# The last stores of a one-core attention and feed-forward kernel, issued in row parts, and its last block copied out by two engines

## The chip, the core and the metric

The kernel runs on one core of a Trainium2 chip. A core has five engines with an instruction queue each: TensorE (PE, matrix products; its weight loads are shown as PEld), VectorE (DVE), ScalarE (ACT), GpSimd (POOL) and SyncE (SP), which computes nothing here and only waits and issues transfers. Sixteen DMA engines move data between the core's buffers and the memory on the chip (DRAM). Engines wait for each other, and for transfers, on semaphores. The metric is the device time of one execution in microseconds (us); lower is better.

## The reference

Two stages follow one another (batch 4, 8 heads, 768 positions, head size 64). First a block-sorted attention, then a feed-forward layer with a squared ReLU over 3072 tokens:

```
P = sort_net, five times normalised by rows and by columns (after exp)
k_sorted, v_sorted = P @ blocks of k, P @ blocks of v
attn_out = softmax(q @ k_sorted.T / 8) @ v_sorted        # within each block of 96
x = attn_out as [3072 tokens, 512]
out = relu(x @ w_in) ** 2 @ w_out                        # w_in [512, 2048], w_out [2048, 512], out [3072, 512] f32
```

## The kernel before, in words

A planner (`Plan`) collects all operations with costs and due times, simulates the engines' queues and emits each engine's instructions in the order that it found. A wait between instructions of two engines is put in by the framework, which follows who reads and writes each buffer. Transfers issued by SP count up on eight semaphores in turn, named DMAHW0 to DMAHW7: the first transfer takes DMAHW0, the ninth takes it again. At the end of the program SP waits for all of them in that order, one or two semaphores to an instruction, and then all engines meet.

The part that matters is the end of the feed-forward layer. The tokens of one batch (768) are two groups of 384. `Group.up` makes the hidden layer of a group, 128 hidden units at a time. The second product (hidden layer times `w_out`) is done for the last batch in three pairs of 128-token blocks. A `Pair` multiplies a 2x2 block matrix by Strassen's scheme in Winograd's form: seven products instead of eight, each of eight matmuls (`product`), numbered by `step(k)` with k = 1, 2, 5, 6, 3, 7, 4, between sums and evictions on DVE and ACT. The first pair of a batch (here P) runs among the `up` steps. The other two, A and B, run last, in this order of steps:

```
steps("1A 2A 1B 2B 5A 6A 5B 6B 3A 7A 3B 7B 4A 4B", A=Pair((g1, 2), (g2, 0)),
      B=Pair((g2, 1), (g2, 2), last=b == B - 1))
```

A name such as 5B below is the product of step 5 of pair B. The sums that a pair needs are in DVE's queue (line 1178), the evictions at lines 1210, 268 and 270.

Each product goes into one of four PSUM banks (bank_71 to bank_74), and a bank is taken again when its eviction is done. A pair fills two output buffers of 128 rows by 512 columns in f32, `o1` for its upper row block and `o2` for its lower one. There are four of them, `ob0` to `ob3` (in the built program ob_166 to ob_169), taken in turn: P has ob_168 and ob_169, A has ob_166 and ob_167, and B has ob_168 and ob_169 again. Before an engine writes into a buffer of the turn before, it waits until the old store from it has landed.

The evictions that the text names: `c11` and `c12` (left and right half of `o1`, after steps 2 and 3), `c22` (right half of `o2`, after step 7) and `c21` (left half of `o2`, after step 4, the last product of a pair). Step 4 adds onto the bank that `c22` has just read, so product 4B waits for `c22` of B; 5B is written into the bank that `c11` of B has emptied. `put` stores a buffer when both halves are there; for the last pair (`last`) the two halves of `o2` are stored apart.

Of the kernel before, what the change touches and what calls it, by code (L numbers as in the profile page):

```python
# [59 lines left out]
X_PE = {1: (0, 1, 2, 3), 2: (0, 1, 2, 3)}  # L60

FIRST_MIX = ("0T 1T 2T 1A 3T 2A 6A 5A 7A 3A 4A", "0T 1T 2T 1A 3T 2A 6A 5A 7A 3A 4A")
PRIO = {"evict": -3, "relu": -2, "square": -1, "sum": 0.5, "T1": 0, "T2": 0.3, "T3": 0.6, "T4": 0.7}


# [129 lines left out]
def kernel(  # L195
# [12 lines left out]
    B, H, S, D = q.shape  # L208
# [8 lines left out]
    d_model = moe_w_in.shape[0]  # L217
# [20 lines left out]
    banks = [psb.tile([128, 512], FP32, name=f"bank{n}") for n in range(4)]  # L238
# [11 lines left out]
    plan = Plan()  # L250
# [15 lines left out]
    def copy(eng, out, in_):  # L266
        if eng == "ACT":
            nc.scalar.copy(out=out, in_=in_)  # L268
        else:
            nc.vector.tensor_copy(out=out, in_=in_)  # L270
# [131 lines left out]
    while w >= 4:  # L402
        dst = {C0: mask, 4: mask_t}.get(w)
        if dst is None:
            dst = const.tile([128, w], BF16, name=f"fold{w}")
# [161 lines left out]
    class Unit:  # L567


        def __init__(self, b, hp, halves):  # L570
            self.b, self.hp, self.halves = b, hp, halves
            self.turned = []
            self.tiled = in_tiles(b, 1, HP * (hp // 2))
            self.n, self.old = rks.take()
            if self.tiled:
                self.ksT = kvT_r[self.n][:, 0, :]
                self.i0, self.ni, self.full = 0, NB, True
                return
            self.kvT = kvT_r[self.n]
            self.ksT, self.vsT = self.kvT[:, 0, :], self.kvT[:, 1, :]  # L580
            self.i0, self.ni = NQ * halves[0], NQ * len(halves)
            self.full = len(halves) == 2
# [455 lines left out]
    ob_r = [const.tile([128, d_model], FP32, name=f"ob{n}") for n in range(4)]  # L1038

    def store(so, dst, src, deps, parts=(slice(0, 128),)):  # L1040
        for p in parts:
            sp = plan.add("SP", 0.55, lambda e, p=p: nc.sync.dma_start(out=dst[p, :], in_=src[p, :]),
                          deps)
        rob.use(so, plan.add("WAY", 1.5, lambda e: None, [sp], tail=0.6))
# [8 lines left out]
    NH2, DH = NT // 2, d_model // 2  # L1053
# [15 lines left out]
    def make_t():  # L1069
# [7 lines left out]
        for h in range(2):  # L1077
            done = []
            for name, dst, x, y in (("T1", T1, B12, B11), ("T2", T2, B22, T1),
# [6 lines left out]
                    readers[0] + lands + dep))  # L1086
                done[-1].prio = PRIO[name]
                tsum.setdefault(name, []).append(done[-1])
# [20 lines left out]
    class Group:  # L1109
# [9 lines left out]
        def up(self, nt):  # L1119
# [6 lines left out]
            def mm(e):  # L1126
# [9 lines left out]
                out=h1_r[:, s1, :], in_=banks[n][:, 0:HS], func=AF.Relu), [pe] + old1)  # L1136
            r.prio = PRIO["relu"]
            fb.use(n, pe, r)
# [20 lines left out]

    class Pair:  # L1160

        def __init__(self, top, low, last=False):
            (g1, m1), (g2, m2) = top, low
            x1, x2 = slice(128 * m1, 128 * (m1 + 1)), slice(128 * m2, 128 * (m2 + 1))
            self.gs, self.last = (g1, g2), last
            self.row1, self.row2 = g1.t0 + x1.start, g2.t0 + x2.start
            A11, A12 = g1.h2[:, 0:NH2, x1], g1.h2[:, NH2:, x1]
            A21, A22 = g2.h2[:, 0:NH2, x2], g2.h2[:, NH2:, x2]
            self.ns, olds = rs3.take()
            S3 = s3_r[self.ns]  # L1170
            self.S = (A11, A12, A21, A22, S3)
            nk, oldk = rkeep.take()
            self.nk = nk
            (self.P1s, d1), (self.U2s, d2), (self.P5s, d5) = keep_r[3 * nk:3 * nk + 3]
            self.oldk = oldk + d1 + d2 + d5

            def add(dst, x, y, op, deps):
                o = plan.add("DVE", 0.68, lambda e: nc.vector.tensor_tensor(  # L1178
                    out=dst, in0=x, in1=y, op=op), deps)
                o.prio = PRIO["sum"]  # L1180
                return o

            self.s3 = add(S3, A11, A21, ALU.subtract, g1.sq[0:NH2] + g2.sq[0:NH2] + olds + readers[0]
                          + [units[1, hp].k_op for hp in range(2) if self.ns == 1])
            self.s1 = add(A21, A21, A22, ALU.add, [self.s3] + g2.sq)
            self.add = add
            self.ops = {}
            self.o1, old1 = rob.take()
            self.o2, old2 = rob.take()
            self.oldo = {1: old1, 2: old2}  # L1190
# [14 lines left out]
        def evict(self, n, dst, deps, other=None):  # L1205
# [7 lines left out]
            fb.use(n, op)  # L1213
            return op

        def step(self, k):
            A11, A12, A21, A22, S3 = self.S
            top, low = (slice(0, DH), slice(DH, d_model))
            o = self.ops
            if k == 1:  # L1220
                self.a, old = fb.take()
                o[1] = self.product(A11, B11, self.a, self.gs[0].sq[0:NH2] + old, True)
                self.p1 = self.evict(self.a, self.P1s, [o[1]] + self.oldk)
                self.s2 = self.add(A11, A21, A11, ALU.subtract, [self.s1, self.s3, o[1]])
            elif k == 2:
                self.b, old = fb.take()
                o[2] = self.product(A12, B21, self.b, self.gs[0].sq + old, True)
                self.c11 = self.evict(self.b, ob_r[self.o1][:, top], [o[2], self.p1] + self.oldo[1],
                                      self.P1s)
                fb.release(self.b)  # L1230
                self.s4 = self.add(A12, A12, A11, ALU.subtract, [self.s2, o[2]])
            elif k == 5:
                self.b, old = fb.take()
                o[5] = self.product(A21, T1, self.b, [self.s1] + tsum["T1"] + old, True)
                self.p5 = self.evict(self.b, self.P5s, [o[5]] + self.oldk)
            elif k == 6:
                o[6] = self.product(A11, T2, self.a, [self.s2, self.p1] + tsum["T2"], False)
                self.u2 = self.evict(self.a, self.U2s, [o[6]] + self.oldk)
            elif k == 3:
                o[3] = self.product(A12, B22, self.b, [self.s4, self.p5], False)  # L1240
                self.c12 = self.evict(self.b, ob_r[self.o1][:, low], [o[3], self.u2], self.U2s)
                fb.release(self.b)
                rkeep.use(self.nk, self.c12)
                self.put(self.o1, self.row1, [self.c11, self.c12], ())
            elif k == 7:
                o[7] = self.product(S3, T3, self.a, [self.s3, self.u2] + tsum["T3"], False)
                rs3.use(self.ns, o[7])
                self.c22 = self.evict(self.a, ob_r[self.o2][:, low], [o[7], self.p5] + self.oldo[2],
                                      self.P5s)
                rkeep.use(self.nk, self.c22)  # L1250
            else:
                o[4] = self.product(A22, T4, self.a, [self.c22] + tsum["T4"], False)
                self.c21 = self.evict(self.a, ob_r[self.o2][:, top], [o[4]])
                fb.release(self.a)
                self.put(self.o2, self.row2, [self.c22, self.c21], (low, top))

        def put(self, so, row, ops, halves):
            dst = out[row:row + 128, :]
            if self.last and halves:
                for x, op in zip(halves, ops):  # L1260
                    store(so, dst[:, x], ob_r[so][:, x], [op])
            else:
                store(so, dst, ob_r[so], ops)

    class Tile:

# [25 lines left out]
    def steps(names, **pairs):  # L1292
        for k in names.split():
            pairs[k[1]].step(int(k[0]))

    def ffn_first():

        make_t()
        for half in range(2):
            g = Group(half)  # L1300
            for nt in range(NT):
                g.up(nt)
            steps(FIRST_MIX[half], T=Tile(g, 2 if half == 0 else 0),
                  A=Pair((g, 0), (g, 1)) if half == 0 else Pair((g, 1), (g, 2)))
        fb.release(3)

    def ffn_batch(b):
        g1, g2 = Group(2 * b), Group(2 * b + 1)
        for nt in range(NT):
            g1.up(nt)  # L1310
        nt = 0
        for k in (None, 1, 2, 5, 6, 3, 7, 4, None):
            for _ in range(3 if nt == 0 else 2):
                if nt < NT:
                    g2.up(nt)
                    nt += 1
            if k == 1:
                p = Pair((g1, 0), (g1, 1))
            if k:
                p.step(k)  # L1320
        steps("1A 2A 1B 2B 5A 6A 5B 6B 3A 7A 3B 7B 4A 4B", A=Pair((g1, 2), (g2, 0)),
              B=Pair((g2, 1), (g2, 2), last=b == B - 1))

    qops = {}
# [3 lines left out]
    for k in range(2):  # L1328
        op = plan.add("DVE", 0.42, lambda e, k=k: p_last(e, k), [step])
# [15 lines left out]
    for name in FIRST.split():  # L1345
        stage, n = name[0], int(name[1])
# [82 lines left out]
    fb = Banks((f_slot[0], f_slot[1], 3 - f_slot[0] - f_slot[1]))  # L1429
# [44 lines left out]
```

## Time and profile before

| | us |
|---|---|
| time, median of 3 runs | 212.22 (212.06 to 214.27) |
| time of the profiled execution | 214.04 |
| span of the profiled execution, first to last instruction | 212.3 |
| PE busy in the span | 205.9 (97%) |
| last product on PE, and last copy after it | 206.98 + 1.91, then 208.92 + 0.37 |
| last store issued on SP | 209.32 |

The profile is of one execution, whose own time is 1.74 us more than its span and 1.82 us more than the median of the other runs. Times inside it are us from the start of its span. A row of a timeline gives start, duration, engine, line, operation and what it writes and reads; a number in brackets at its end is the idle time of the engine before it and what ended it. The names of buffers are without their numbers there (ob for ob0 to ob3).

### The profile page before, as it was taken

The numbers are of one execution on the slowest core, as the hardware profiler recorded it, in microseconds if no ns is written. First come the engines' busy times: TensorE is split into PE (matmuls) and PEld (weight loads), VectorE is DVE, ScalarE is ACT, GpSimd is POOL, SyncE is SP. The second block draws the span as 40 slices with busy tenths as digits, with TensorE's granted clock in tenths as the row PEclk, the third lists the DMA queues.
The fourth block names the chain that finished last, engine by engine and source line by source line (L and its number), as shares of the span: only waits on it lengthen the run. The fifth ranks groups of instructions, "written<-read, shape, count | busy, mean of one in ns | idle before, by whom it ended". The sixth has DMA issues, their size and how long they took to land.

```text
span 212.3 us, 5721 instructions
## 1 busy us (share of the span) xinstructions
PE 205.9 (97%) x2337; PEld 143.7 (68%) x2340; DVE 141.2 (67%) x309; ACT 150.4 (71%) x307; POOL 30.8 (15%) x57
## 2 busy tenths in 40 slices
PE   8999999999999999999999999989999999999993
PEld 2467666576566865566779955556789865677882
DVE  5849589974779846867798747677879314633920
ACT  4578799548994549999884089999672189887321
POOL 7957222000019000000720000000000000000000
PEclk9999999999999999999999999999999999999999
DMA  6999999999697994299599768953432420001113
GB/s 142 218 202 208 204 207 211 192 220 280 158 195 134 202 252 85 65 173 185 153 183 229 147 225 113 190 134 96 64 115 40 136 99 0 3 0 49 53 49 148
DMA packets 42266, 30.57 MB, mean 144 GB/s; under 512 B 21696, under 2 KB 37312, under 8 KB 42240
## 3 DMA queue, kind: packets, MB, share of 16 engines
q0 software_dynamic: 12224, 13.24, 37.6%
q1 hardware_dynamic: 30016, 16.97, 33.7%
q8 instruction: 18, 0.29, 0.5%
q14 instruction: 8, 0.07, 0.1%
HBM read 29.70 MB, written 8.72 MB: 181 GB/s over the span
## 4 chain that ended last, share of the span: by engine, by line
PE 89%; ACT 4%; DMA 2%; DVE 2%; issue 1%; ACTq 0%; POOLq 0%
PE bank L1128 36%; PE bank L1195 31%; PE p L945 4%; PE p L718 3%; PE bank L1278 3%; PE p L476 2%; DMA qb<-in_q_dram 2%; ACT h_r L1135 2%; PE p L806 2%; DVE h L1152 1%; PE bank L597 1%; PE bank L998 1%; PE bank L768 1%; PE bank L644 1%; PE p L680 1%
## 5 line engine op out<-in xcount | busy, mean ns | idle before, releaser
L1128 PE MATMUL bank<-xT,w_in_bf 128*128 128x384 bf16 x506 | 90.7, 326 | 0.0
L1128 PEld LDWEIGHTS <-w_in_bf 128*128 128x128 bf16 x506 | 47.1, 98 | 29.1 <-issue 1.4
L1135 ACT ACTIVATE h_r<-bank 128x384 f32<-128x384 f32 x128 | 59.8, 497 | 8.2 <-PE bank L1128 7.1
L1195 PEld LDWEIGHTS <-h 128*128 128x128 bf16 x528 | 50.1, 98 | 9.1 <-issue 1.0
L1152 DVE TENSOR_TENSOR h<-h_r 128x768 bf16<-128x768 f32 x28 | 26.6, 957 | 20.2 <-ACT h_r L1135 20.1
L1195 PE MATMUL bank<-w_out_bf,h 128*128 128x256 bf16 x264 | 33.1, 273 | 0.1
L1150 ACT ACTIVATE h<-h_r 128x768 bf16<-128x768 f32 x36 | 30.6, 851 | 0.9
L749 ACT ACTIVATE et<-p 96x384 bf16<-96x384 f32 x48 | 22.2, 504 | 2.9 <-PE p L718 2.9
L956 DVE TENSOR_TENSOR ao<-p,rec 96x512 bf16<-96x512 f32 x32 | 22.0, 687 | 1.1
L1178 DVE TENSOR_TENSOR h<-h 128x1024 bf16<-128x1024 bf16 x30 | 20.1, 684 | 0.7 <-ACT h L1150 0.5
L1195 PE MATMUL bank<-qb,h 128*128 128x256 bf16 x132 | 17.9, 272 | 0.0
L268 ACT COPY ob<-bank 128x256 f32<-128x256 f32 (+1 forms) x11 | 4.5, 411 | 18.6 <-PE bank L1195 17.4
L268 ACT COPY qT<-bank 128x256 f32<-128x256 f32 (+1 forms) x22 | 8.9, 413 | 10.5 <-PE bank L1195 7.9
L1210 DVE TENSOR_TENSOR ob<-bank,kvT 128x256 f32<-128x256 f32 x18 | 7.6, 424 | 10.5 <-PE bank L1195 9.0
L945 PEld LDWEIGHTS <-et 96*128 96x128 bf16 x256 | 11.1, 97 | 2.8 <-issue 0.7
L268 ACT COPY kvT<-bank 128x256 f32<-128x256 f32 x14 | 5.2, 371 | 10.1 <-PE bank L1195 10.1
L476 PE MATMUL p<-ones 128*128 128x512 bf16 (+1 forms) x28 | 10.2, 524 | 1.1 <-DVE ones L294 1.1
L1195 PE MATMUL bank<-vb,h 128*128 128x256 bf16 x88 | 11.1, 273 | 0.0
L1210 DVE TENSOR_TENSOR ob<-bank,qT 128x256 f32<-128x256 f32 x15 | 6.2, 422 | 7.2 <-PE bank L1195 5.8
L1412 POOL COPY held<-kx 1x1 bf16<-1x1 bf16 x6 | 1.7, 286 | 58.3 <-DMA kx<-kn 58.3
L718 PEld LDWEIGHTS <-kvT 64*128 64x128 bf16 x256 | 6.4, 94 | 5.4 <-issue 4.2
L945 PE MATMUL p<-vblk,et 96*128 96x65 bf16 x192 | 8.9, 193 | 0.0
(109 smaller groups left out, 227.1 us busy)
## 6 DMA issues: line engine op xcount, KB each, us to landing
out_dram<-ob SPq DMA_DIRECT2D x23, 256.0 KB, 2.2
v_way<-vn SPq DMA_DIRECT2D x6, 396.0 KB, 4.9
vblk<-v_way SPq DMA_DIRECT2D x6, 396.0 KB, 4.1
vb<-in_v_dram POOLq DMA_DIRECT2D x6, 384.0 KB, 11.5
kb<-in_k_dram POOLq DMA_DIRECT2D x6, 384.0 KB, 10.3
qb<-in_q_dram POOLq DMA_DIRECT2D x6, 384.0 KB, 12.9
w_in_bf<-in_moe_w_in_dram POOLq DMA_DIRECT2D x4, 512.0 KB, 12.2
w_out_bf<-in_moe_w_out_dram POOLq DMA_DIRECT2D x4, 512.0 KB, 15.7
```

Source lines behind the costliest of these rows:

```text
L268: nc.scalar.copy(out=out, in_=in_)
L476: nc.tensor.matmul(out=p2[slot][:, 0, 0:128 * r].rearrange("p (r x) -> p r x", r=r), lhsT=ones, rhs=ones[:, None, :].to_broadcast([128, r, ...
L749: nc.scalar.activation(out=et[:, h, 0:HS].rearrange("p (n c a) -> p n c a", c=C0, a=NA), in_=st["p"][0:96, h, 0:HS].rearrange("p (n a c) - ...
L945: nc.tensor.matmul(out=oup[:, h, 66 * n:66 * n + D + 1], lhsT=et_r[u.et[hf]][:, h, BLK * n:BLK * n + 128], rhs=(u.vs[:, NQ * hf + n, h, 0: ...
L956: nc.vector.tensor_tensor(out=u.ao[:, n0:n0 + NQ, :, :].rearrange("p n e d -> p e n d"), in0=ov[:, :, :, 0:D], in1=rec[:, :, :, None].to_b ...
L1128: nc.tensor.matmul(out=banks[n][:, 0:HS], lhsT=w_in_bf[:, kc, 128 * nt:128 * (nt + 1)], rhs=xT[:, kc, t0:t0 + HS], start=(kc == 0), stop=( ...
L1135: r = plan.add("ACT", cost_f(HS)[0], lambda e: nc.scalar.activation(out=h1_r[:, s1, :], in_=banks[n][:, 0:HS], func=AF.Relu), [pe] + old1)
L1150: nc.scalar.activation(out=h2, in_=h1, func=AF.Square)
L1152: nc.vector.tensor_tensor(out=h2, in0=h1, in1=h1, op=ALU.mult)
L1178: o = plan.add("DVE", 0.68, lambda e: nc.vector.tensor_tensor(out=dst, in0=x, in1=y, op=op), deps)
L1195: nc.tensor.matmul(out=banks[n][:, 0:DH], lhsT=a[:, j, :], rhs=b[j] if isinstance(b, list) else b[:, j, :],  start=(start and j == 0), sto ...
L1210: op = plan.add("DVE", cost_f(DH)[1], lambda e: nc.vector.tensor_tensor(out=dst, in0=src, in1=other, op=ALU.add), deps)
```

## The change

For the last batch, the stores of P go out in three row parts each (42, 43 and 43 rows), and the store of A's `o1` in two (64 and 64 rows); A's `o2` and B's stores stay as they were. That is five transfers more, so the last store takes DMAHW7 where it took DMAHW2. The last eviction of the kernel (`c21` of B, 128 rows by 256 columns) is written as two copies of 128 columns, one for ACT and one for DVE.

```
+LAST_PARTS = (3, 3), (2, 1)
...
-        def __init__(self, top, low, last=False):
+        def __init__(self, top, low, last=False, parts=(1, 1)):
...
+        def last_evict(self, deps):
+            ops = []
+            for e, x in (("ACT", slice(0, DH // 2)), ("DVE", slice(DH // 2, DH))):
+                ops.append(plan.add(e, 0.28, lambda e, x=x: copy(
+                    e, ob_r[self.o2][:, x], banks[self.a][:, x]), deps))
+                ops[-1].prio = PRIO["evict"]
+            fb.use(self.a, *ops)
+            return ops
...
-                self.c21 = self.evict(self.a, ob_r[self.o2][:, top], [o[4]])
+                if self.last:
+                    c21 = self.last_evict([o[4]])
+                else:
+                    c21 = [self.evict(self.a, ob_r[self.o2][:, top], [o[4]])]
...
+            n = self.parts[so == self.o2]
+            store(so, dst, ob_r[so], ops + more,
+                  [slice(128 * i // n, 128 * (i + 1) // n) for i in range(n)])
...
-                p = Pair((g1, 0), (g1, 1))
+                p = Pair((g1, 0), (g1, 1), parts=LAST_PARTS[0] if b == B - 1 else (1, 1))
...
+              A=Pair((g1, 2), (g2, 0), parts=LAST_PARTS[1] if b == B - 1 else (1, 1)),
```

In SP's queue the stores of the last batch stood as follows, at the end of the program. ob_168 and ob_169 are first those of P, and further down those of B; ob_166 and ob_167 are A's. Of the waits of a row the first is for the semaphore that the transfer itself will count on.

```order
L1042 DMA out_dram<-ob_168 128x512 [waits DMAHW4_49,DVE_49]
L1042 DMA out_dram<-ob_169 128x512 [waits DMAHW5_49,DVE_49]
L1042 DMA out_dram<-ob_166 128x512 [waits DMAHW6_49,DVE_49]
L1042 DMA out_dram<-ob_168 128x512 [waits DMAHW7_49,DVE_49]
L1042 DMA out_dram<-ob_169 128x256 [waits DMAHW0_49,DVE_49]
L1042 DMA out_dram<-ob_167 128x512 [waits DMAHW1_49,Activation_49]
L1042 DMA out_dram<-ob_169 128x256 [waits DMAHW2_49,Activation_49]
```

The same place of SP's queue in the changed kernel:

```order
L1043 DMA out_dram<-ob_168 42x512 [waits DMAHW4_49,DVE_49]
L1043 DMA out_dram<-ob_168 43x512 [waits DMAHW5_49]
L1043 DMA out_dram<-ob_168 43x512 [waits DMAHW6_49]
L1043 DMA out_dram<-ob_169 42x512 [waits DMAHW7_49,DVE_49]
L1043 DMA out_dram<-ob_169 43x512 [waits DMAHW0_49]
L1043 DMA out_dram<-ob_169 43x512 [waits DMAHW1_49]
L1043 DMA out_dram<-ob_166 64x512 [waits DMAHW2_49,DVE_49]
L1043 DMA out_dram<-ob_166 64x512 [waits DMAHW3_49]
L1043 DMA out_dram<-ob_168 128x512 [waits DMAHW4_49,DVE_49]
L1043 DMA out_dram<-ob_169 128x256 [waits DMAHW5_49,DVE_49]
L1043 DMA out_dram<-ob_167 128x512 [waits DMAHW6_49,Activation_49]
L1043 DMA out_dram<-ob_169 128x256 [waits DMAHW7_49,DVE_49]
```

No row is moved; three rows have become eight, and the last row waits for DVE instead of ACT (called Activation in these rows) and counts on DMAHW7.

The end of DVE's queue before: `c11` of B into ob_168, a sum, `c12` of A (into ob_166), `c22` of A (ob_167), `c12` of B and `c22` of B (ob_169).

```order
L1210 TENSOR_TENSOR ob_168<-bank_73,kvT_88 128x256 [waits DMAHW4_49,PE_49,Activation_49]
L1178 TENSOR_TENSOR h_1_165<-h_1_165 128x8x128 [waits DVE_49]
L1210 TENSOR_TENSOR ob_166<-bank_74,qT_84 128x256 [waits PE_49,Activation_49]
L1210 TENSOR_TENSOR ob_167<-bank_71,qT_85 128x256 [waits DMAHW3_49,PE_49]
L1210 TENSOR_TENSOR ob_168<-bank_73,kvT_96 128x256 [waits PE_49,Activation_49]
L1210 TENSOR_TENSOR ob_169<-bank_72,kvT_104 128x256 [waits DMAHW5_49,PE_49]
```

The same place in the changed kernel:

```order
L1211 TENSOR_TENSOR ob_168<-bank_73,kvT_88 128x256 [waits DMAHW5_49,DMAHW4_49,DMAHW6_49,PE_49,Activation_49]
L1179 TENSOR_TENSOR h_1_165<-h_1_165 128x8x128 [waits DVE_49]
L1211 TENSOR_TENSOR ob_166<-bank_74,qT_84 128x256 [waits PE_49,Activation_49]
L1211 TENSOR_TENSOR ob_167<-bank_71,qT_85 128x256 [waits DMAHW3_49,PE_49]
L1211 TENSOR_TENSOR ob_168<-bank_73,kvT_96 128x256 [waits PE_49,Activation_49]
L1211 TENSOR_TENSOR ob_169<-bank_72,kvT_104 128x256 [waits DMAHW1_49,DMAHW7_49,DMAHW0_49,PE_49]
L271 COPY ob_169<-bank_72 128x128 [waits Activation_49]
```

`c11` and `c22` of B now wait for three parts each instead of one store, and a copy of 128 columns, which waits for ACT alone, has come behind them. In ACT's queue the last row, `COPY ob_169<-bank_72`, goes from 128x256 to 128x128 in its place.

More of the change, by code (lines that the diff above doesn't have):

```diff
@@ L1160 @@
     class Pair:
-        def __init__(self, top, low, last=False):
+        def __init__(self, top, low, last=False, parts=(1, 1)):
             (g1, m1), (g2, m2) = top, low
             x1, x2 = slice(128 * m1, 128 * (m1 + 1)), slice(128 * m2, 128 * (m2 + 1))
-            self.gs, self.last = (g1, g2), last
+            self.gs, self.last, self.parts = (g1, g2), last, parts
             self.row1, self.row2 = g1.t0 + x1.start, g2.t0 + x2.start
@@ L1243, in step @@
                 rkeep.use(self.nk, self.c12)
-                self.put(self.o1, self.row1, [self.c11, self.c12], ())
+                self.put(self.o1, self.row1, [self.c11], [self.c12])
             elif k == 7:
@@ L1252, in step, with put @@
                 o[4] = self.product(A22, T4, self.a, [self.c22] + tsum["T4"], False)
-                self.c21 = self.evict(self.a, ob_r[self.o2][:, top], [o[4]])
+                if self.last:
+                    c21 = self.last_evict([o[4]])
+                else:
+                    c21 = [self.evict(self.a, ob_r[self.o2][:, top], [o[4]])]
                 fb.release(self.a)
-                self.put(self.o2, self.row2, [self.c22, self.c21], (low, top))
-        def put(self, so, row, ops, halves):
+                self.put(self.o2, self.row2, [self.c22], c21)
+        def put(self, so, row, ops, more):
             dst = out[row:row + 128, :]
[L1259 to L1263, printed above, removed]
+            if self.last and so == self.o2:
+                for x, deps in ((slice(DH, d_model), ops), (slice(0, DH), more)):
+                    store(so, dst[:, x], ob_r[so][:, x], deps)
+                return
+            n = self.parts[so == self.o2]
+            store(so, dst, ob_r[so], ops + more,
+                  [slice(128 * i // n, 128 * (i + 1) // n) for i in range(n)])
     class Tile:
@@ L1317, in ffn_batch @@
             if k == 1:
-                p = Pair((g1, 0), (g1, 1))
+                p = Pair((g1, 0), (g1, 1), parts=LAST_PARTS[0] if b == B - 1 else (1, 1))
             if k:
                 p.step(k)
-        steps("1A 2A 1B 2B 5A 6A 5B 6B 3A 7A 3B 7B 4A 4B", A=Pair((g1, 2), (g2, 0)),
+        steps("1A 2A 1B 2B 5A 6A 5B 6B 3A 7A 3B 7B 4A 4B",
+              A=Pair((g1, 2), (g2, 0), parts=LAST_PARTS[1] if b == B - 1 else (1, 1)),
               B=Pair((g2, 1), (g2, 2), last=b == B - 1))
```

## Prediction

> **What bounds the kernel now.** First the page's busy times, then the last pieces of the chain that ended last, then the timeline of each engine behind the last matmul.
>
> ```profile
> PE 205.9 (97%) x2337; PEld 143.7 (68%) x2340; DVE 141.2 (67%) x309; ACT 150.4 (71%) x307; POOL 30.8 (15%) x57
> 195.05 0.65 PE bank L1128 x4
> 195.70 13.20 PE bank L1195 x120
> 208.90 0.02 issue
> 208.92 0.37 ACT ob L268
> ```
>
> PE is busy throughout and ends without a gap: 120 matmuls in 13.20 us are fifteen products (4 of P, then the fourteen of A and B) of 0.87 to 0.88 us. So only two things move the time: what makes PE wait in these 13.2 us, and what lies between its last matmul and the end of the span.
>
> The second part, from the timelines of ACT and SP, SP's end-of-program instructions (line 1469) over 209.66 to 211.43, over 211.03 to 211.05, and over 211.40 to 211.43, and the last store alone:
>
> ```profile
> 208.92 0.37 ACT L268 COPY ob<-bank 128x256 f32<-128x256 f32 x1 [0.50 <-PE bank L1195]
> 209.32 0.33 SPq L1042 DMA_DIRECT2D out_dram<-ob  x1
> L1469 SPq EVENT_SEMAPHORE  x9: 28/28/28, 209.7 to 211.3; - x9
> L1469 SPq EVENT_SEMAPHORE  x1: 28/28/28, 211.0 to 211.0; - x1
> L1469 SPq DRAIN  x1: 13/13/13, 211.4 to 211.4; - x1
> DMA to landing us min/median/max: 1.7/1.7/1.7
> ```
>
> The copy ends at 209.29, SP issues 0.03 later, the store lands 1.7 later, and its wait ends at 211.04. SP then goes through the rest of its nine waits, the last at 211.3, and drains at 211.4 (within 211.40 to 211.43). Barriers fill the rest up to 212.3. About 3.4 us lie behind the last matmul, of which the change can touch 0.4 (the copy) and 0.4 (211.04 to 211.41).
>
> **The end of the program.** The nine waits go through DMAHW0 to DMAHW7 in order, and the last store held DMAHW2, so five waits stand behind it that had nothing left to wait for. From 211.04 to 211.41 are six steps (five waits and the drain), 0.06 each. With DMAHW7 in the last place the five are done earlier, while SP waits anyway: 5 x 0.06 = **-0.30**.
>
> **The last copy.** The nearest rows by form: an ACT copy of 128 columns out of a bank, and two DVE widths for the slope.
>
> ```profile
> L1336 ACT CAST pt<-bank 128x128 bf16<-128x128 f32 x2 | 0.4, 268 | 0.1
> L1210 DVE TENSOR_TENSOR ob<-bank,kvT 128x256 f32<-128x256 f32 x18 | 7.6, 424 | 10.5 <-PE bank L1195 9.0 <-ACT h L1150 1.3
> L956 DVE TENSOR_TENSOR ao<-p,rec 96x512 bf16<-96x512 f32 x32 | 22.0, 687 | 1.1
> ```
>
> 256 columns more cost DVE 263 ns, so 128 fewer than 256 cost 424 - 131 = 293 ns. In DVE's queue the new copy waits for ACT, not for PE, and ACT's last instruction that it can wait for after product 4B is its own half copy. The halves therefore run one behind the other: 0.27 + 0.03 (the step that the timeline shows from ACT's end to SP's start) + 0.29 = 0.59 instead of 0.37: **+0.22**. Together with the term before, -0.08; if that were all, the change would be worth nothing.
>
> **The row parts.** What they can cost depends on when the old stores land, because pair B takes P's two buffers again. DVE and PE there, from their timelines:
>
> ```profile
> 193.37 16.28 SPq L1042 DMA_DIRECT2D out_dram<-ob  x7
> 196.70 0.42 DVE L270 COPY ob<-bank 128x256 f32<-128x256 f32 x1 [0.52 <-PE bank L1195]
> 200.64 0.42 DVE L1210 TENSOR_TENSOR ob<-bank,kvT 128x256 f32<-128x256 f32 x1
> 200.98 0.68 DVE L1178 TENSOR_TENSOR h<-h 128x1024 bf16<-128x1024 bf16 x1
> 207.18 0.42 DVE L1210 TENSOR_TENSOR ob<-bank,kvT 128x256 f32<-128x256 f32 x1 [0.38 <-PE bank L1195]
> 202.61 1.04 PE L1195 MATMUL bank<-qb,h 128*128 128x256 bf16 x8
> 205.23 1.04 PE L1195 MATMUL bank<-w_out_bf,h 128*128 128x256 bf16 x8
> 206.98 1.91 PE L1195 MATMUL bank<-vb,h 128*128 128x256 bf16 x16
> ```
>
> P's first store is issued at 193.37, its second when `c21` of P ends, at 197.15. `c11` of B (200.64) needs the first landed, `c22` of B (207.18) the second. Product 5B, which takes the bank of that `c11`, starts one product before 6B (202.61), at 201.74. 4B starts one product after 4A (206.98), at 207.85, and needs `c22` (done at 207.60).
>
> The price of a transfer: the one store of 196.50 to 199.50, by windows and by the DMA view of the same stretch, and the landing of the seven stores of this stage.
>
> ```profile
> 196.50:199.50 3.00, 3.00 (x30) 2.69 (x28) 2.72 (x6) 1.17 (x3) 0.00 (x0) 1.00 0.22 87
> DMA packets 144, 0.26 MB, mean 87 GB/s; under 512 B 16, under 2 KB 16, under 8 KB 144
> q1 hardware_dynamic: 144, 0.26, 22.4%
> L1042 SPq DMA_DIRECT2D out_dram<-ob x7: 332/332/333, 193.4 to 209.3; - x7
> DMA to landing us min/median/max: 1.7/2.0/2.0
> ```
>
> 128 rows made 128 packets of 2 KB and 16 tiny ones, one for each DMA engine. 22.4% of 16 engines over 3.0 us are 10.75 engine-us, 84 ns a row. Eight rows an engine are 0.67 of the 2.0 to landing; the other 1.33 is fixed. An issue takes 0.33; I put the next one 0.38 later (estimate).
>
> No transfer of before has 42 or 43 rows, so the trace has no price for such a part, only two ends.
>
> - Cheap end: 43 rows are spread as three an engine. The last part of P's first store is issued at 194.13 and landed by 196.2, 4.4 us before `c11`; that of the second by 199.9, 7.3 before `c22`. All of it is hidden. Total -0.08.
> - Dear end: a part is dealt out in equal shares or not at all. The only pattern that the rows show is equal shares: eight rows and one end packet for each of 16 engines. 43 has no divisor up to 16 but 1, so a part of 43 rows would go through one engine; 42 go to 14 engines, three rows each.
>
> I take the dear end, since equal shares are all that the rows show. The four parts of 43 rows then stand in line on the same engine:
>
> - First buffer: two parts, 86 x 0.084 = 7.22. The second part is issued at 193.75; landed at 193.75 + 1.33 + 7.22 = 202.30 (the first two terms, 195.08, come back below) instead of 195.4. `c11` of B starts at 202.33, ends at 202.75, and 5B starts at 202.78 instead of 201.74: **PE stands for 1.04**. The sum behind `c11` on DVE (200.98) ends at about 203.4, ahead of 3B (205.23, now 206.3), so nobody else is late.
> - Second buffer: behind the first, 86 + 3 + 86 = 175 rows, 14.7. Landed at 193.75 + 1.33 + 14.7 = 209.78. `c22` of B, by then ready from PE at 207.18 + 1.04 = 208.22, starts at 209.81 and ends at 210.23. 4B starts at 210.26 instead of 207.85: **+2.41**, the first stand included.
> - The later stores find that engine free by 209.8, and B's second is issued only after `c22`; A's parts of 64 rows are four rows on each engine. Nothing of theirs is late.
>
> [...]
>
> **Sum.** 2.41 + 0.22 - 0.30 = **+2.33**. The profiled execution would go from 214.04 to 216.4 and its span from 212.3 to 214.6. The median of the runs is 1.82 below the profiled execution, and what the sum uses lies at the end, in every execution alike: 212.22 + 2.33 = **214.5**.
>
> **The rivals.**
>
> - The parts are spread over all engines, and only the end changes: 212.22 - 0.08 = 212.1. For it: the landing of every store is within 0.3 of 2.0. Against it: all of those have 128 rows. This one ends not slower, and it decides as soon as a row on the line costs under (200.64 - 195.08) / 86 = 0.065.
> - One engine, but faster when it alone is at work. Under (208.22 - 195.08) / 175 = 0.075 a row PE's second stand falls to what the first left, and the total to about +0.75: 213.0. Against it: 84 ns is the engine's own busy time, not a wait for others.
> - One engine and slower, 0.090 a row: 4B at 211.3, total +3.4: 215.6. Instruction fetches on the same engine would do that.
> - The two halves of the last copy run side by side after all, with spread parts: 0.29 instead of 0.59, so 211.8. Against it: the wait of DVE's copy names ACT alone.
>
> **How the numbers follow.** One engine for 43 rows: 0.75, with its own range from 213.0 to 215.6. Spread parts: 0.20. Everything else, copies side by side among it: 0.05. The range takes in the first two cases: 212.0 to 215.6. About 1% is what a measurement of this kernel can tell from no change; that is 2.12 us, just under my sum. Of the 0.75 I put 0.50 above that line and 0.25 below; with 0.18 of the spread parts and 0.02 of the rest, no change has 0.45, slower 0.52 (0.50 and 0.02 for unforeseen waits), and faster by over 1% gets 0.03, since no term that gains exceeds 0.4.
>
> **What would show it.** Landing of P's parts: about 8.2 us for the third of the first buffer, 11.9 for the third of the second, against 2.0. In PE's timeline a gap of about 1.0 before 5B and another of about 1.4 before 4B; in the chain DMA as what `c11` and `c22` of B wait for. At the end DVE's copy behind ACT's, the last store 1.7 to landing, and no waits between its landing and the drain. Gaps missing and landings near 2 us would make the prediction wrong at the dear end; gaps of another size, at the price of a row.

## The result, and the profile after

The changed kernel takes 216.32 us (median of 6 runs, 215.72 to 216.57) against 212.22 us before (212.06 to 214.27): a ratio of 1.0175, 95% interval 1.015 to 1.0199. It is slower by 1.5 to 2.0%, where the forecast was 214.5 and its range ended at 215.6. The ratio is worked out over all runs of both kernels and makes 3.7 us; the two medians lie 4.1 apart, but before's median was 212.48 to 212.76 in the three later comparisons, so its 212.22 was a little low. The profiled execution of after took 215.72, its span is 213.9.

The page first: the busy times, and the main pieces of the chain that ended last from product 4 of P on.

```profile
span 213.9 us, 5733 instructions
PE 204.0 (95%) x2340; PEld 142.9 (67%) x2340; DVE 141.8 (66%) x310; ACT 150.3 (70%) x307; POOL 32.2 (15%) x57
194.17 0.97 PE bank L1196 x8
196.27 12.71 DMA out_dram<-ob
209.18 0.43 DVE ob L1211
209.66 1.05 PE bank L1196 x8
210.72 0.28 ACT ob L269
211.02 0.29 DVE ob L271
```

Where before had one piece of 13.20 us of PE, a store now carries 12.71 us of the path. Behind it come `c22` of B on DVE, the eight matmuls of 4B, and the two copy halves one behind the other. (The lines named here stand one higher than before: L1043, L1196 and L1211 are the old L1042, L1195 and L1210. Only the end-of-program line, 1488, is the old 1469.)

PE's and DVE's timelines show the two stands. The bracket at a row's end is how long the engine sat idle ahead of it, and whom it waited for.

```profile
194.09 1.03 PE L1196 MATMUL bank<-vb,h 128*128 128x256 bf16 x8
202.41 0.60 PE L1196 MATMUL bank<-qb,h 128*128 128x256 bf16 x4 [2.05 <-DVE ob L1211]
209.66 1.03 PE L1196 MATMUL bank<-vb,h 128*128 128x256 bf16 x8 [0.97 <-DVE ob L1211]
201.93 0.42 DVE L1211 TENSOR_TENSOR ob<-bank,kvT 128x256 f32<-128x256 f32 x1 [2.75 <-DMA out_dram<-ob]
209.18 0.42 DVE L1211 TENSOR_TENSOR ob<-bank,kvT 128x256 f32<-128x256 f32 x1 [1.71 <-DMA out_dram<-ob]
211.02 0.29 DVE L271 COPY ob<-bank 128x128 f32<-128x128 f32 x1 [1.42 <-ACT ob L269]
```

PE waits 2.05 ahead of 5B for `c11` of B, and `c11` waits for the parts of P's first store. It waits 0.97 ahead of 4B for `c22` of B, and `c22` waits for the parts of the second. From the start of product 4 of P (194.09) to the end of 4B (209.66 + 1.03) pass 16.60 us. In the trace of before the same products run from 195.63 to 208.89 (206.98 + 1.91, in the prediction's fence), 13.26 us:

```profile
195.63 1.03 PE L1195 MATMUL bank<-vb,h 128*128 128x256 bf16 x8
```

The difference, 3.34, is the two stands and about 0.17 more for each of them, because an undisturbed product's row overlaps the next one's by 0.17.

The end, from SP's timeline and its end-of-program instructions (line 1488) over 211.7 to 213.1 and over 213.04 to 213.20:

```profile
211.34 0.33 SPq L1043 DMA_DIRECT2D out_dram<-ob  x1
L1488 SPq EVENT_SEMAPHORE  x9: 17/28/28, 211.7 to 213.1; - x9
L1488 SPq EVENT_SEMAPHORE  x1: 28/28/28, 213.1 to 213.1; - x1
L1488 SPq DRAIN  x2: 7/7/7, 213.1 to 213.2; - x2
```

The store is issued 0.03 after DVE's copy ends, and its wait, 1.7 later, is the last of the nine: the drain follows at once, where before five waits stood between.

Executions of either kernel reach this stage up to 1.8 us apart, most of it from their first 15 us, and the profiled execution of before was a late one; sums are therefore taken from product 4 of P on. A second profile of before shows it (the product alone, and the chain's last piece of PE):

```profile
193.94 1.03 PE L1195 MATMUL bank<-vb,h 128*128 128x256 bf16 x8
194.02 13.20 PE bank L1195 x120
```

It begins this stage 1.69 earlier and takes the same 13.20 for it. So 3.34 us are lost in the stage and 0.12 won at the end (3.25 us from the last product to the end of the span instead of 3.37), 3.22 in all; the ratio makes 3.7 of 212.22. The rest is taken up under `after_third`.

### The profile page after: what moved, and what is told of

The parts are those of the page before. It is cut to its first block, busy times and chain, and to the rows that moved or that the text cites. A ratio compares the mean times of both kernels' runs of the same rounds, so it can differ in the third digit from the quotient of the medians.

```text
span 213.9 us, 5733 instructions
## 1 busy us (share of the span) xinstructions
PE 204.0 (95%) x2340; PEld 142.9 (67%) x2340; DVE 141.8 (66%) x310; ACT 150.3 (70%) x307; POOL 32.2 (15%) x57
## 4 chain that ended last, share of the span: by engine, by line
PE 82%; DMA 8%; ACT 4%; DVE 2%; issue 1%; SPq 0%; DVEq 0%; ACTq 0%; POOLq 0%
PE bank L1129 35%; PE bank L1196 26%; DMA out_dram<-ob 6%; PE p L946 4%; PE p L719 3%; PE bank L1296 3%; DMA qb<-in_q_dram 2%; ACT h_r L1136 2%; PE p L477 2%; PE p L807 2%; DVE h L1153 1%; PE bank L598 1%; PE bank L999 1%; PE bank L769 1%; PE bank L645 1%
## 5 line engine op out<-in xcount | busy, mean ns | idle before, releaser
L1196 PEld LDWEIGHTS <-h 128*128 128x128 bf16 x528 | 50.1, 98 | 12.5 <-issue 4.2
L1196 PE MATMUL bank<-w_out_bf,h 128*128 128x256 bf16 x264 | 33.1, 273 | 0.1
L1196 PE MATMUL bank<-qb,h 128*128 128x256 bf16 x132 | 18.0, 272 | 2.0 <-DVE ob L1211 2.0
L269 ACT COPY ob<-bank 128x256 f32<-128x256 f32 (+2 forms) x11 | 4.4, 401 | 19.8 <-PE bank L1196 14.5
L1211 DVE TENSOR_TENSOR ob<-bank,kvT 128x256 f32<-128x256 f32 x18 | 7.6, 425 | 14.1 <-PE bank L1196 8.2
L1196 PE MATMUL bank<-vb,h 128*128 128x256 bf16 x88 | 11.2, 273 | 1.0 <-DVE ob L1211 1.0
L1431 POOL COPY held<-kx 1x1 bf16<-1x1 bf16 x6 | 2.9, 486 | 57.7 <-DMA kx<-kn 57.7
L1211 DVE TENSOR_TENSOR ob<-bank,qT 128x256 f32<-128x256 f32 x15 | 6.3, 422 | 6.6 <-PE bank L1196 5.2
L477 PE MATMUL p<-ones 128*128 128x512 bf16 (+1 forms) x28 | 8.0, 430 | 1.1 <-DVE ones L295 1.1
```

Source lines behind the costliest of these rows:

```text
L1196: nc.tensor.matmul(out=banks[n][:, 0:DH], lhsT=a[:, j, :], rhs=b[j] if isinstance(b, list) else b[:, j, :],  start=(start and j == 0), sto ...
L1211: op = plan.add("DVE", cost_f(DH)[1], lambda e: nc.vector.tensor_tensor(out=dst, in0=src, in1=other, op=ALU.add), deps)
```

## The experiments

All of them use the same stage sum: start of product 4 of P to end of 4B, 13.26 in before and 16.60 in after. `before_again`, `after_again` and `after_third` are the two kernels unchanged. The others start from the changed kernel; those that cut the row parts anew do it with this edit, and only the two tuples for three parts differ (the first is for P's second buffer, `o2`, the other for its first):

```
-            n = self.parts[so == self.o2]
+            cuts = {1: (0, 128), 2: (0, 64, 128), 3: (0, 48, 96, 128) if so == self.o2 else (0, 48, 96, 128)}[self.parts[so == self.o2]]
 ...
-                  [slice(128 * i // n, 128 * (i + 1) // n) for i in range(n)])
+                  [slice(x, y) for x, y in zip(cuts, cuts[1:])])
```

**The two kernels once more.**

> The kernel before once more, for its trace. In its first profile product 4 of P ended at 196.67 and the span was 212.3; in that of the changed kernel it ended at 195.14, though nothing differs ahead of it. If the first profile of before was one of the late executions (214.0 against 212.2), this one ends that product at about 194.9, its span is 210.4 and its time 212.2, and the distance from there to the end of the last product is 12.23 again. If the changed kernel is really 1.5 faster ahead of the pairs, the product ends at 196.7 again and the span is 212.3.

> The changed kernel once more, for its trace. Theory 1 (the parts of 43 rows in line on one engine): landing of P's parts again about 9.5 and 11 us, PE stands of about 2 us before 5B and 1 us before 4B, 3.3 together; the time between 215.7 and 216.6. If its time is nearer 216.5, the stands are longer by what it lies above 215.7, or product 4 of P ends later than 195.1, or matmuls after the stand take longer than 0.87 a product; the trace tells which.

`before_again` took 212.32 and its stage 13.26. `after_again` took 215.47, a little under its range, and its stage 16.60, with the same two stands, from PE's timeline:

```profile
202.19 0.60 PE L1196 MATMUL bank<-qb,h 128*128 128x256 bf16 x4 [2.08 <-DVE ob L1211]
209.40 1.03 PE L1196 MATMUL bank<-vb,h 128*128 128x256 bf16 x8 [0.94 <-DVE ob L1211]
```

**Parts of 48, 48 and 32 rows** (`3: (0, 48, 96, 128)`): as many transfers and waits, but each count of rows has 16 as a divisor.

> P's stores cut at rows 48 and 96, so parts of 48, 48 and 32 rows; as many transfers, and all else as in the changed kernel. Theory 1 (43 rows go through one engine): all parts land in about 2 us, no stand before 5B or 4B, time -0.08 against before, 212.1. Rival (more transfers as such delay the landing, or the two copies and the end cost the time): the stands stay, 215 to 216.5.

212.95 (12 runs), ratio 1.0013, interval 0.9982 to 1.0045. The chain's last pieces, and the landing of P's six parts:

```profile
195.71 13.20 PE bank L1196 x120
208.93 0.28 ACT ob L269
209.23 0.29 DVE ob L271
DMA to landing us min/median/max: 1.8/1.9/2.0
```

PE's 13.20 in one piece are back. Three transfers in place of one make PE wait for nothing here; only the row counts differ from the changed kernel.

**The same, with the last block copied by ACT alone** (`-if self.last:` / `+if False:` ahead of the call of `last_evict`), run twice.

> The same with parts of 48, 48 and 32 rows, and the last block copied by ACT alone as before. Theory 1: -0.30 against before, 211.9, and 0.2 faster than the kernel with the two copies, whose halves run one behind the other. Rival (the two copies gain): 0.1 to 0.2 slower than that kernel.

> Parts of 48, 48 and 32 rows and one copy by ACT, once more to narrow the interval: five waits fewer at the end, -0.30, a ratio of 0.9986.

212.19 and 212.53 (12 runs each); ratios 0.9977 (0.9948 to 1.0005) and 0.9987 (0.9958 to 1.0017). The end of the chain in the first of them:

```profile
193.94 13.20 PE bank L1196 x120
207.16 0.37 ACT ob L269
```

From the last product's end to the end of the span are 3.07 us instead of 3.37 in before: the -0.30 of the five waits is there. The times can't tell it from no change. This is the best version found, and it doesn't measurably beat before.

**The copy in halves alone** (stores whole: `LAST_PARTS = (1, 1), (1, 1)`).

> No row parts, so the last store takes DMAHW2 as before; only the last block is copied by ACT and DVE. The two halves one behind the other: from the end of product 4B to the issue of the last store 0.64 instead of 0.42, and from its landing to the drain five waits as before; +0.22 from the end of 4B to the end of the span. Rival (the halves overlap): 0.34 to the issue, -0.08.

212.72 (one run). The copy on ACT, its other half on DVE from the chain, and SP's issue of the last store:

```profile
207.40 0.27 ACT L269 COPY ob<-bank 128x128 f32<-128x128 f32 x1 [0.50 <-PE bank L1196]
207.69 0.29 DVE ob L271
208.01 0.33 SPq L1043 DMA_DIRECT2D out_dram<-ob  x1
```

DVE begins when ACT ends. From copy to issue 0.61 instead of 0.40, +0.21, and from the last product to the span's end 3.57 instead of 3.37.

**Equal shares, but fewer engines** (`3: (0, 40, 84, 128)`, parts of 40, 44 and 44 rows).

> P's stores cut at rows 40 and 84, so parts of 40, 44 and 44 rows, none a multiple of 16. Equal shares over the largest possible number of engines: 10, 11 and 11 engines, four rows each; every part lands in about 2 us, no stand, -0.08 against before. Rival (a row count that is no multiple of 16 goes through one engine): the stands of the changed kernel, 3.3 together.

212.33 (10 runs), ratio 0.9978 (0.9942 to 1.0014), no stand, the stage 13.26. So it is neither the number of parts nor a count that is no multiple of 16. The number of engines of a part can be counted. The DMA view of the stretch with these six parts (192 to 200):

```profile
DMA packets 321, 0.54 MB, mean 68 GB/s; under 512 B 64, under 2 KB 64, under 8 KB 320
```

Beside 256 rows and one packet of another queue there are 64 tiny ones, the end packets, one for each engine of a part: 2 x (10 + 11 + 11). The semaphores say the same. But for one step at the issue of a part on fewer than 16 engines, they step once for each engine whose rows have landed: 10 times for 40 rows here, 11 for 44, in the other traces 14 for 42, 13 for 13, 16 for 32, 48 and 64, and once for 43 and for 73. Ten or eleven engines do as well as sixteen, and what is left is the count of rows that falls to one engine.

**One buffer only in thirds of 42, 43 and 43.** First P's first store (the second in 48, 48 and 32), then the other way round.

> Only P's first buffer in parts of 42, 43 and 43 rows; its second in 48, 48 and 32. Theory 1 (43 rows on one engine, in line): PE stands 2.05 to 2.1 before 5B as in the changed kernel; the second buffer has three rows a part on that engine, behind the line that ends at about 201.8, so it is landed by 202.6 and 4B does not wait. From the end of product 4 of P to the end of 4B 12.23 + 2.2 = 14.4, total +2.1 against before. Rival (each stand comes from its own buffer alone): the same first stand, so this run only bounds the second: 0.9 to 1.1 less than the changed kernel's 15.57.

> Only P's second buffer in parts of 42, 43 and 43 rows; its first in 48, 48 and 32. Theory 1: the line on one engine is 86 rows of 0.080, so it lands 8.2 after the issue of the second part, 9.1 after the end of product 4 of P, or 10.2 if the stops of 1.1 us in the changed kernel's first part come with the start of any line; c22 of B needs it at 10.5. No stand, -0.08 against before, 212.1 to 212.4. Rival (a buffer's own parts make its own stand): 4B waits about 1 us, total +1. The packets tell whether the stops belong to the start of a line: if they do, some of the first rows take 0.25 to 0.6 each; if they come from something else between 193 and 196, there are none.

`second_only`: 212.97 (10 runs), ratio 1.0001 (0.9959 to 1.0043), no stand: two parts on one engine alone are hidden, if barely (they landed at 205.20, and `c22` of B started 0.10 later than its product alone allowed, which PE's next product did not feel). `first_only`: 216.31 (4 runs), ratio 1.0158 (1.0113 to 1.0203). Expected was +2.1 against before, and it is +1.58%, or 3.4: a miss, for the loss is nearly that of the whole change although the second stand is gone as expected. PE's timeline from 5B on, and windows of 1 us (their length; busy and instructions of PE, PEld, DVE, ACT, POOL; then the clock that TensorE was granted, DMA share, GB/s):

```profile
202.16 0.60 PE L1196 MATMUL bank<-qb,h 128*128 128x256 bf16 x4 [2.04 <-DVE ob L1211]
204.37 1.92 PE L1196 MATMUL bank<-w_out_bf,h 128*128 128x256 bf16 x8
206.07 1.41 PE L1196 MATMUL bank<-kb,w_all 128*128 128x256 bf16 x8
202.00:203.00 1.00, 0.84 (x8) 0.76 (x8) 0.71 (x2) 0.00 (x0) 0.00 (x0) 1.00 0.00 0
203.00:204.00 1.00, 1.00 (x9) 0.77 (x8) 0.00 (x0) 0.37 (x1) 0.00 (x0) 0.70 0.00 0
204.00:205.00 1.00, 1.00 (x6) 0.70 (x5) 0.00 (x0) 0.37 (x1) 0.00 (x0) 0.50 0.00 0
206.00:207.00 1.00, 1.00 (x8) 0.72 (x7) 0.43 (x1) 0.00 (x0) 0.00 (x0) 0.59 0.00 0
207.00:208.00 1.00, 1.00 (x12) 0.90 (x10) 0.42 (x1) 0.00 (x0) 0.00 (x0) 1.00 0.00 0
```

The granted clock falls to 0.50 at 203.4, 1.2 us after the stand has ended, and is back at 206.8, 3.4 us later. Products of 1.04 take up to 1.92. The stage takes 17.13: 13.26 + 2.21 for the stand (2.04 and the overlap) leaves 1.66, and about 3.4 us at half speed lose 1.7. So a stand of 2.04 cost 3.87.

**The changed kernel a third time, timed by itself**, to see whether its runs have this too.

> The changed kernel in more executions. Theory 2 (the rest of the loss is TensorE's clock: a stand of 2 us that falls into one stretch of the gate's 3.41 us halves the clock for the next 3.41 us): executions with a mean clock of 0.997 or more take 215.4 to 215.8, those at 0.990 to 0.992 take 216.2 to 216.6. The slow clock costs 1.7 to 1.8 in the products behind 5B, of which 0.95 would have been spent waiting before 4B anyway, so 0.8 is left. If the profiled execution is one of them, its PE wait before 4B is gone or nearly so and PEclk is 0.5 over 3.4 us. Rival (the stands themselves vary): times go with the length of the stands, at a clock of 1.0.

216.94 (4 runs), ratio 1.0177 (1.0112 to 1.0242). The expectation on the clock is met, since all four executions have a mean of 0.990 to 0.992; that on the times is missed, since two of the four took 216.0 and two 217.8 to 217.9, none of them 216.2 to 216.6; the traced one, of 217.84, began product 4 of P at 195.6, 1.7 late. The trace, from PE's timeline, its waits (in all, times, longest) and one window:

```profile
203.97 0.60 PE L1196 MATMUL bank<-qb,h 128*128 128x256 bf16 x4 [2.07 <-DVE ob L1211]
206.32 1.91 PE L1196 MATMUL bank<-w_out_bf,h 128*128 128x256 bf16 x8
PE bank L1196 <- DVE ob L1211: 2.1, 1, 2.1
206.00:207.00 1.00, 1.00 (x7) 0.69 (x6) 0.00 (x0) 0.37 (x1) 0.00 (x0) 0.50 0.06 25
```

Here the slow stretch takes the place of the second stand: PE comes to 4B so late that P's second buffer has landed before `c22` of B needs it. The stage is 17.16, 0.56 more than without the drop. Of the six executions behind the result three had a mean clock of 0.990 to 0.992, as here (216.3 to 216.6), and three had 0.995 to 0.997 (215.7 to 216.3). That would put part of them at 3.22 and part at 3.8 over before, around the 3.7 of the ratio. A mean of 0.992 needs a whole slow stretch: 1.7 of 214 us is 0.008, while the drop at the idle end of the program, at 212.34 in after, leaves 0.996. Still this is argued: of the six only that of 215.72 has a trace, and it has no drop in this stage; and 3 of the 63 executions of before behind the experiments, and 2 of the 10 of `second_only`, have such a mean too, without a stand that a trace shows.

**A lone part of 73 rows** (`3: (0, 42, 115, 128)` for the first buffer, 48, 48 and 32 for the second): one part on one engine, with nothing of that kind behind it.

> P's first store cut at rows 42 and 115 (42, 73 and 13 rows: 14, 1 and 13 engines), its second in 48, 48 and 32. Theory 1: the line on one engine is 73 rows instead of 86 (and one row of the last part), so the stand before 5B is 13 x 0.080 shorter than 2.05: 1.0 to 1.1. Theory 2: a stand of that length doesn't halve the clock, so the mean clock is 0.997 or more in every execution and the time is +1.0 against before, 213.2 to 213.6, three below the run with only the first buffer in parts of 43 rows. The stops at the start of the line, 1.1 together, stay if they belong to its start; they go if they came from issuing a second part onto the same engine.

213.92 (10 runs), ratio 1.0053 (1.0019 to 1.0087). The stand, from PE's timeline:

```profile
201.90 0.60 PE L1196 MATMUL bank<-qb,h 128*128 128x256 bf16 x4 [1.11 <-DVE ob L1211]
```

1.11 of the 1.0 to 1.1 expected; the stage takes 14.53, and the clock never fell in it (mean 0.998 or more in all ten executions). The time is above the 213.2 to 213.6 expected, but the ratio makes +1.1 of the +1.0. So the price of a line on one engine holds for another length, and the clock's loss is no part of a short stand.

## Why the prediction was wrong, step by step

**Direction and mechanism: right.** Parts of 43 rows went through one engine, the parts of both buffers in line; `c11` and `c22` of B waited for them and PE for those two. The rival of spread parts fell with the two stands, and `sixteens` and `forty_fours` leave nothing else to carry them. Choosing the dear end on the pattern of equal shares alone was a step without a row for 43; the runs bear it out. On how a transfer is dealt out the Trainium skill, "DMA: Bandwidth & Descriptors", section "Why a DMA increments its semaphore by 16 and not by 1", says that it uses the largest number of engines up to 16 that divides the slowest dimension of both sides. The runs side with it: parts of 43 and of 73 rows landed through one engine, 40, 44 and 48 caused no stand. P's parts landed 9.25 us (third of the first buffer) and 12.72 us (third of the second) after their issue, where 8.2 and 11.9 were forecast.

**The end: right.** Waits -0.30 (measured -0.30), copy +0.22 (+0.21); the sum was -0.08 and is -0.12 (3.25 instead of 3.37 behind the last product in `sixteens`).

**The failed step: the price of the line on one engine, "fixed 1.33 + 84 ns a row".** The prediction had `c11` of B start 8.96 after the first part's issue, and `c22` 16.44 after it. SP issued the first part at 191.83 (the row of its timeline below), so with DVE's rows above it is 201.93 - 191.83 = 10.10 and 209.18 - 191.83 = 17.35. Both are late by about one amount, 1.14 and 0.91, so the loss is made once, not for each row. Below that row stands the DMA view of two stretches of after, each with its packets and the share of 16 engines that they took: first 193.60 to 195.70, where the line begins, then 202.20 to 205.20:

```profile
191.83 0.38 SPq L1043 DMA_DIRECT2D out_dram<-ob  x1
DMA packets 12, 0.02 MB, mean 12 GB/s; under 512 B 0, under 2 KB 0, under 8 KB 12
q1 hardware_dynamic: 12, 0.02, 6.0%
DMA packets 39, 0.08 MB, mean 26 GB/s; under 512 B 1, under 2 KB 1, under 8 KB 39
q1 hardware_dynamic: 39, 0.08, 6.7%
```

6.0% of 16 engines over 2.1 us are 2.0 engine-us for 12 packets, 168 ns each; 6.7% over 3.0 are 3.2 for 39, 82 ns each. A running line is thus as cheap as the prediction said, a little under 84. Its start is dear: 12 x (168 - 82) = 1.0 us of packets that take several times their share (273, 398 and 588 ns), or 1.2 with one of 255 that begins just ahead of the stretch. All six traces with such a line have three to five packets of 247 to 598 ns in its first 2.5 us, `second_only` too, 3 us later, and `one_73` with no second line behind it; so they go with the start of a line, not with a moment of the program. What stops the engine there stays open.

From the issue of the second part (192.26) to the last step of the semaphores (201.81 and 208.99) the line took 9.55 and 16.73, instead of the predicted 8.55 and 16.03. On the running line a row starts 80 ns after the one before it, 4 less than predicted, which takes 0.3 and 0.7 off; the start adds the 1.2, and the 0.1 to 0.2 left over lie in the fixed 1.33. The rest of the 1.14 and 0.91 is the issue (0.43 behind the first, estimated at 0.38) and the step from the landing to DVE, which now goes through three waits (0.12 and 0.19, predicted 0.03).

The rival "0.090 a row" had the right direction but the wrong place. By it the first stand would be 1.04 + 86 x 0.006 = 1.6 and the second 1.9, and they are 2.05 and 0.97. That its total, +3.4, comes near the 3.22 of the trace is luck. With the start of the line as above, the first stand is longer by about 1.0, and the second is then smaller than forecast (0.97, not 1.4), as the first has moved PE further.

**The missing step: the clock.** No term of the prediction had PE slower after it had stood. Where the clock fell, a stand of 2.04 cost another 1.66, or 0.56 where it swallowed the second stand. With the stage at +3.34 instead of +2.41, the sum is 3.22 instead of 2.33, and 212.22 + 3.22 = 215.4 would still have been inside the range; what lies beyond is put down in part to this, and in part to the executions' different starts, which is argued (see `after_third`).

**From profile to median.** The prediction took its change as the same in every execution, and added it to the median. That the stage of before has 13.26 in both of its traces bears it out for before; for after it failed, because whether the clock falls differs between executions of the same kernel (the last section shows on what it hangs).

## What to carry to other kernels

Before a transfer is cut by rows, look at the row count of each part: parts of 43 or 73 rows went through one engine at 26 GB/s and cost 0.5 to 1.75% where their buffer was taken again too soon, while parts of 40, 44 or 48 rows cost nothing that the times can tell. What such a part delays shows not at its issue but where the buffer is taken again, 10 and 14 us after the store's first issue here. A stand of PE near 2 us is to be priced with the clock that may fall behind it: 2.04 came to 3.87 in one execution, and 2.05 to no more than the stand in another.

## What was not expected of the hardware

**The clock after a short stand.** A gap of 2.04 to 2.07 us was followed by 3.4 us at half clock (`first_only`, `after_third`); one of 2.08 in `after_again` and of 2.05 in after was not, and neither was 1.11 in `one_73`. The Trainium skill, "TensorE: Matmul & The Clock Gate", section "Part 1: The HAM clock gate (the "warmup" mystery)", tells of an idle window of about 3.4 us ahead of a drop. The length of the slow stretch agrees with that (3.4), the gap that sufficed does not, and here the measurement decides.

Why like gaps ended differently can be read from the traces, which record each change of the granted clock. In `first_only` these are at 5.43 (to full), 203.41 (to half), 206.82 (to full) and 213.65 (to half), in `after_third` at 10.51, 205.07, 208.48 and 215.31. The distances are 58, 1 and 2 times 3.413 us, and 57, 1 and 2 times; in every trace with more than one change they are such multiples. So the clock changes on a grid of 3.413 us, whose place differs from execution to execution. Counted on from the first change, the grid has these stretches with the gap, by windows: those of `first_only` and `after_third`, then, with the larger part of the gap, those of after and `after_again` (length, then the time PE was busy):

```profile
199.99:203.41 3.42, 1.38 (x14) 1.12 (x12) 1.02 (x2) 0.55 (x2) 0.00 (x0) 1.00 0.04 14
201.65:205.07 3.42, 1.35 (x14) 1.05 (x12) 1.02 (x2) 0.40 (x2) 0.00 (x0) 1.00 0.07 26
198.69:202.10 3.41, 1.67 (x16) 1.35 (x14) 0.67 (x2) 0.74 (x2) 0.00 (x0) 1.00 0.06 25
201.05:204.47 3.42, 2.29 (x21) 2.05 (x21) 1.02 (x2) 0.71 (x2) 0.00 (x0) 1.00 0.07 26
```

Where the whole gap fell into one stretch, PE was idle for 2.04 and 2.07 of it, and the clock fell at its end; where the grid cut the gap, for at most 1.74 and 1.13, and it did not. From the first rise of the clock to the end, the ends of the programs included, no stretch of the 13 traces with PE idle for 1.93 us or less has a drop behind it, and each with 2.04 or more that ends within the span has one. No run moved the gap alone to test it.

**An issue that blocks.** With three parts of 43 rows already in line on that engine, SP's issue of the second buffer's third part took 1.40 us instead of 0.24 to 0.41 for the other five (the row of issues over 196.2 to 197.7, min, median and max in ns); it is 1.42 and 1.40 in the two other traces of the kernel. Nothing waited behind it.

```profile
L1043 SPq DMA_DIRECT2D out_dram<-ob x2: 255/825/1395, 196.0 to 196.3; - x2
```

**The first 15 us.** The same kernel reaches product 4 of P up to 1.8 us earlier or later. In the first 10 us the matmuls of one line differ, here in before and then in `before_again` (durations in ns, min, median and max; first and last start):

```profile
L476 PE MATMUL p<-ones x7: 609/634/635, 7.0 to 9.5; 128*128 128x512 bf16 x7
L476 PE MATMUL p<-ones x12: 379/379/389, 3.9 to 8.3; 128*128 128x512 bf16 x12
```

It is the clock that comes up later. The first change on record, to full clock, is at 10.26 in before and at 3.72 in `before_again`, and these matmuls go from 634 to 379 ns there; the windows, which take an execution's clock as full until its first change, don't show it. In the three traces where it lies at 10.2 to 10.5 (before, `sixteens`, `after_third`) product 4 of P starts at 195.6, in the ten where it lies at 3.7 to 6.5 at 193.7 to 194.5.
